# Query transposes moved from TensorE to the DMA crossbar, x products as block-diagonal matmuls, and a reordered start, in an attention-plus-FFN kernel

## Chip, cores, metric

One core of a Trainium2 chip. The metric is device time in microseconds (us) of the slowest core, here the only one; lower is better. In the profiles PE is TensorE, ACT ScalarE, DVE VectorE, POOL GpSimd and SP the sync engine; a line with `SPq` shows how long a DMA issue holds SP's queue, and a transfer's landing is the arrival of its data. A verdict compares two kernels in rounds on the same chip. Ratios are the mean time of one kernel's runs over that of the other's runs of the same rounds, so they are not quite the ratio of the medians quoted beside them.

## The reference

```python
# q, k, v: (8 batches, 8 heads, 576 tokens, 64) float32
q_s = softmax(q, axis=-1)                 # over the 64 features
k_s = softmax(k, axis=2)                  # over the 576 tokens
kv  = einsum('bhsd,bhse->bhde', k_s, v)   # 64 x 64 per head
attn = einsum('bhsd,bhde->bhse', q_s, kv)
x = attn.transpose(0, 2, 1, 3).reshape(4608, 512)
a = x @ w1;  b = x @ w2                   # 512 x 1024 each
out = ((a * b) @ w3) @ w_out              # 1024 x 1024, 1024 x 512
```

## The kernel before

It works in float16 with float32 sums. W3 @ W_out is computed once ("the W3 phase"), so that each chunk of 512 tokens needs only two sums for a and b ("s1") and one for the output ("s2"). Batches of attention (576 tokens) are prepared between the sums of earlier chunks. A batch needs, for each half of its heads (`i`): exponentials and a division, a transpose of the normalised queries, kv, and x. The parts that matter here (`pc` holds the pieces of batch 1, `s2(j, tb)` is the output sum of 128 tokens of a chunk; cuts marked `# ...`):

```python
def load_w12(wi, qt):                     # one quarter of w1 or w2: one 512 KB load
    t = slot([P, N_CT, 256])
    w = (moe_w1, moe_w2)[wi]
    nc.sync.dma_start(
        out=t, in_=w.rearrange("(c p) f -> p c f", p=P)[:, :, qt * 256:(qt + 1) * 256])
    w32[(wi, qt)] = t

def piece_t(b, i):                        # nine 128x128 transposes on TensorE, one copy
    pt = pAtt([P, R, P], F16)
    for r in range(R):
        nc.tensor.transpose(pt[:, r, :], eqns[(b, i)][:, r].rearrange("p h d -> p (h d)"), ident)
    qsT = attn.tile([P, 2, R, SP], F16, tag="qsT", name="qsT", bufs=3)
    nc.vector.tensor_copy(out=qsT.rearrange("p g r s -> p r g s"),
                          in_=pt.rearrange("p r (g s) -> p r g s", g=2))
    # ...

def piece_x(b, i, hf, copy=None):         # four 64x64 quadrants of the array
    xp = pAtt([P, 2, 512], F32)
    # ...
    for hh in range(2):
        rows = slice(64 * hh, 64 * hh + 64)
        for g in range(2):
            nc.tensor.matmul(xp[64 * g:64 * g + 64, hh, 0:HS], lhsT=kv2[rows, g, :],
                             rhs=qsT[rows, g, cols], start=True, stop=True)
    # ... copy to xT

# ... after the W3 phase: the second-batch phase, then chunks 1 to 8
pc[0]()                 # transposes of batch 1, first half
s2(0, 0)
pc[1]()                 # second half
s2(0, 1, alt=True)
pc[2]()                 # kv
s2(0, 2)
pc[3]()                 # x
s2(0, 3, alt=True)
pc[4]()                 # x
```

All loads and stores are issued by the sync engine (SP), in program order, on one queue: first batch 0, then w1 and w2, w3 and W_out, batches 1 and 2.

The softmax here doesn't subtract the row's maximum and nothing guards it: scores larger than these inputs give would overflow.

Of the kernel before, what the change touches and what calls it, by code (L numbers as in the profile page):

```python
# [16 lines left out]
def kernel(  # L17
# [11 lines left out]
    nc = tc.nc  # L29
# [10 lines left out]
    HS = S // 2  # L40
# [15 lines left out]
    wosb = [konst.tile([P, 2, C], F16, name=f"wo_{i}") for i in range(4)]  # L56
    W3O = [konst.tile([P, C], F16, name=f"W3O{i}") for i in range(N_FT)]
# [26 lines left out]
    def load_w12(wi, qt):  # L84
        t = slot([P, N_CT, 256])
        w = (moe_w1, moe_w2)[wi]
        nc.sync.dma_start(
            out=t, in_=w.rearrange("(c p) f -> p c f", p=P)[:, :, qt * 256:(qt + 1) * 256])
        w32[(wi, qt)] = t
# [53 lines left out]
    def piece_kv(b, i):  # L143
        kvp = pAtt([P, 2, 512], F32)
        for r in range(R):
            for g in range(2):
                rows = slice(64 * g, 64 * g + 64)
                nc.tensor.matmul(kvp[:, g, 0:130].rearrange("p (h e) -> p h e", h=2),  # L148
                                 lhsT=eks[(b, i)][rows, r].rearrange("p h d -> p (h d)"),
                                 rhs=v16buf[b % 2][rows, 2 * i:2 * i + 2, r, 0:65],  # L150
                                 start=(r == 0), stop=(r == R - 1))
        rc = attn.tile([P, 2], F32, tag="rc", name="rc", bufs=4)
        nc.vector.reciprocal(out=rc, in_=kvp[:, :, 64])
        kv2 = attn.tile([P, 2, D], F16, tag="kv2", name="kv2", bufs=4)
        for hh in range(2):
            sl = slice(64 * hh, 64 * hh + 64)
            nc.vector.tensor_tensor(
                out=kv2[sl], in0=kvp[sl, :, 65 * hh:65 * hh + 64],
                in1=rc[sl, :, None].broadcast_to([64, 2, 64]), op=ALU.mult)
        kvs[(b, i)] = kv2  # L160

    def piece_t(b, i):
        pt = pAtt([P, R, P], F16)
        for r in range(R):
            nc.tensor.transpose(pt[:, r, :], eqns[(b, i)][:, r].rearrange("p h d -> p (h d)"),  # L165
                                ident)
        qsT = attn.tile([P, 2, R, SP], F16, tag="qsT", name="qsT", bufs=3)
        nc.vector.tensor_copy(out=qsT.rearrange("p g r s -> p r g s"),  # L168
                              in_=pt.rearrange("p r (g s) -> p r g s", g=2))
        qsTs[(b, i)] = qsT.rearrange("p g r s -> p g (r s)")  # L170

    def piece_x(b, i, hf, copy=None):
        xp = pAtt([P, 2, 512], F32)
        qsT, kv2 = qsTs[(b, i)], kvs[(b, i)]
        cols = slice(hf * HS, (hf + 1) * HS)
        for hh in range(2):
            rows = slice(64 * hh, 64 * hh + 64)
            for g in range(2):
                nc.tensor.matmul(xp[64 * g:64 * g + 64, hh, 0:HS], lhsT=kv2[rows, g, :],  # L179
                                 rhs=qsT[rows, g, cols], start=True, stop=True)  # L180
        (copy or nc.scalar.copy)(  # L181
            out=xT[:, 2 * i:2 * i + 2, b * S + hf * HS:b * S + (hf + 1) * HS],
            in_=xp[:, :, 0:HS])

    def pieces(b):
        return [lambda: piece_t(b, 0), lambda: piece_t(b, 1),
                lambda: (piece_kv(b, 0), piece_kv(b, 1)),
                lambda: (piece_x(b, 0, 0), piece_x(b, 0, 1)),
                lambda: (piece_x(b, 1, 0), piece_x(b, 1, 1))]
# [9 lines left out]
    def s1(j, fb):  # L199
        t0 = j * CH  # L200
        qt, fo = fb // 2, (fb % 2) * P
        pa = pAB()
        for ct in range(N_CT):
            nc.tensor.matmul(pa, lhsT=w1sb[qt][:, ct, fo:fo + P], rhs=xT[:, ct, t0:t0 + CH],  # L204
                             start=(ct == 0), stop=(ct == N_CT - 1))
        a16 = ffn.tile([P, CH], F16, tag="a16", name="a16", bufs=3)
        nc.scalar.copy(out=a16, in_=pa)
        pb = pAB()
        for ct in range(N_CT):
            nc.tensor.matmul(pb, lhsT=w2sb[qt][:, ct, fo:fo + P], rhs=xT[:, ct, t0:t0 + CH],  # L210
                             start=(ct == 0), stop=(ct == N_CT - 1))
        ab = ffn.tile([P, CH], F16, tag="abT", name="abT", bufs=16)
        nc.vector.tensor_tensor(out=ab, in0=pb, in1=a16, op=ALU.mult)
        abT[(j, fb)] = ab

    outv = out.rearrange("(b s r) c -> b r s c", r=R, s=SP)

    def s2(j, tb, alt=False):
        po = pAtt([P, C], F32) if alt else pO()
        for ft in range(N_FT):  # L220
            nc.tensor.matmul(po, lhsT=abT[(j, ft)][:, tb * P:(tb + 1) * P], rhs=W3O[ft],  # L221
                             start=(ft == 0), stop=(ft == N_FT - 1))
        osb = ffn.tile([P, C], F32, tag="osb", name="osb", bufs=4)
        nc.vector.tensor_scalar(out=osb, in0=po, scalar1=ISC, scalar2=None, op0=ALU.mult)  # L224
        for h in range(2):
            b, rem = divmod(j * CH + tb * P + h * SP, S)
            nc.sync.dma_start(out=outv[b, rem // SP], in_=osb[h * SP:(h + 1) * SP, :])
# [44 lines left out]

    warm(26)
# [10 lines left out]
    load_w3(1)  # L284
# [11 lines left out]
    piece_x(0, 0, 0)  # L296
    piece_x(0, 0, 1)
# [4 lines left out]
    vcopy(out=w1sb[0], in_=w32[(0, 0)])  # L302
    acopy(out=w2sb[0], in_=w32[(1, 0)])
    piece_x(0, 1, 0)
    piece_x(0, 1, 1, vcopy)
# [5 lines left out]
    for ft in range(2, 8):  # L311
        load_w3(ft)
# [5 lines left out]
    for fb in range(N_FT):  # L318
        s1(0, fb)
# [8 lines left out]
        if fb == 6:  # L328
            w3_c(1)
            w3_t(0)  # L330
            vcopy(out=wosb[0], in_=w32[("o", 0)])
            vcopy(out=wosb[1], in_=w32[("o", 1)])
    w3_t(1)
    vcopy(out=wosb[2], in_=w32[("o", 2)])
    vcopy(out=wosb[3], in_=w32[("o", 3)])
    w3_c(2)

    def elementwise_steps(b):
# [5 lines left out]
        for i in range(2):  # L344
            st += [lambda i=i: exp_k(b, i, 0),
                   lambda i=i: (cast_v(b, i, pcopy), exp_k(b, i, 1))]
# [4 lines left out]
    for ft in range(N_FT):  # L351
        w3_m(ft)
        if ft + 3 < N_FT:
            w3_c(ft + 3)
        if ft + 2 < N_FT:
            w3_t(ft + 2)
        for f in {4: ew[0:2], 5: ew[2:5], 6: ew[5:8], 7: ew[8:9]}.get(ft, []):
            f()
    pc[0]()
    ew[9]()  # L360
    ew = elementwise_steps(2)
    s2(0, 0)
    pc[1]()
    s2(0, 1, alt=True)
    ew[0]()
    ew[1]()
    pc[2]()
    ew[2]()
    s2(0, 2)
    ew[3]()  # L370
    pc[3]()
    ew[4]()
    s2(0, 3, alt=True)
    pc[4]()
    ew[5]()
    ew[6]()
    ew[7]()
# [5 lines left out]
    for j in range(1, N_CHUNK):  # L383
        pcs = dict(zip((3, 4, 6, 8, 10) if j == 1 else (0, 1, 3, 5, 7),
# [3 lines left out]
        for n, f in enumerate(steps):  # L388
            ews.setdefault(min(n + 3, 11) if j == 1 else n, []).append(f)
        if j == 1:  # L390
            ews[0] = ew[8:9]
            ews[1] = ew[9:10]
# [12 lines left out]
    for tb in range(4):  # L405
        s2(N_CHUNK - 1, tb, alt=tb % 2)


# [28 lines left out]
```

## Time and profile before

| | before |
|---|---|
| median of 4 runs | 256.9 us |
| span of the profiled run | 255.1 us |
| first sum of s1 starts | 16.8 us |
| W3 phase ends | 50.1 us |
| chunk 1 starts | 63.0 us |
| from one batch-preparing chunk to the next | 23.9 us |

The page of the kernel before. The first two lines are span and busy time. The rest are the span in 40 slices of 6.4 us: busy share of TensorE (PE) in tenths, the clock granted to it in tenths, the DMA engines' busy share in tenths and what they moved. The last line gives shares of the chain of waits by engine.

```profile
span 255.1 us, 4178 instructions
...
PE 243.5 (95%) x1592; PEld 115.6 (45%) x1592; DVE 137.4 (54%) x244; ACT 112.0 (44%) x185; POOL 50.2 (20%) x38
...
PE   8999989897999999999999999999999999999982
...
PEclk9999999999999999999999999999999999999999
DMA  7999999994999219932991497211211321132135
GB/s 247 385 349 368 390 411 391 391 390 121 278 394 391 94 41 302 337 84 43 315 323 42 102 322 258 44 42 41 44 41 41 81 47 41 42 68 58 41 82 123
...
PE 87%; DMA 4%; DVE 3%; ACT 2%; issue 1%; POOL 1%; DVEq 0%; POOLq 0%; ACTq 0%
```

PE is busy nearly everywhere and at full clock, and the chain runs through it for 87% of the span. So time that leaves PE is time won, as long as nothing else takes its place. The DMA line says where that could be: from the second slice to the ninth, up to 57 us, the DMA engines are full, at 349 to 411 GB/s from the third slice on.

PE's timeline in one steady chunk (start, length, line, operation, count): kv (L148), one of the two x groups (L179), both transposes (L165), and the next chunk's kv. The first two lines are earlier: the last pair of matmuls of the W3 phase (L250; with 0.43 us for the two it ends at 50.1) and the first sum of chunk 1 (L204, 63.03).

```profile
49.68 0.59 PE L250 MATMUL po<-wo_86,w3T 128*128 128x512 f16 x2
...
63.03 0.61 PE L204 MATMUL pab<-xT,w_0_75 128*128 128x512 f16 x2
...
113.17 1.21 PE L148 MATMUL att<-v_0_73,ek 64*128 64x130 f16 x36
...
117.87 0.44 PE L179 MATMUL att<-qsT,kv_1532 64*64 64x288 f16 x8
...
130.82 0.67 PE L165 MATMUL att<-ident,eqn 128*128 128x128 f16 x9
...
133.05 0.67 PE L165 MATMUL att<-ident,eqn 128*128 128x128 f16 x9
...
137.10 1.10 PE L148 MATMUL att<-v_1_74,ek 64*128 64x130 f16 x32
```

From kv to kv it is 137.10 - 113.17 = 23.93 us. A nine-fold transpose takes 0.50 us of PE's issue time (from 130.82 to the next sum at 131.32; the printed length includes the end of the pipeline), so two cost 1.0 us a chunk. An x group costs 0.47 us.

The sync queue's timeline: the eight w1/w2 loads and the next loads.

```profile
3.94 13.53 SPq L87 DMA_DIRECT2D st<-in_moe_w_dram  x8
17.56 2.47 SPq L99 DMA_DIRECT2D st<-in_moe_w_dram  x2
```

The w1/w2 loads and their direct figures (least, median and greatest time that one holds the queue, in ns):

```profile
L87 SPq DMA_DIRECT2D st<-in_moe_w_dram x8: 470/1390/3577, 3.9 to 16.1; - x8
```

The shortest such issue took 0.47 us, the median 1.39; what held the longer ones the trace does not show. The times of the phases in the table above are read from PE's timeline in the same way.

### The profile page before, as it was taken

To read this page: it belongs to the slowest core of one execution; us is meant where nothing else is said; L and a number is where in the kernel's file an instruction comes from. 1 tells how busy PE (TensorE), PEld (TensorE's weight loads), DVE (VectorE), ACT (ScalarE), POOL (GpSimd) and SP (SyncE) were. 2 spreads that over 40 slices of the span, in tenths; PEclk is the share of its full clock that TensorE was granted. 3 is DMA by queue.
4 is the path that set the end of the run, shared out by engine and by line. 5 is a ranking of instruction groups with operands and counts; after the bars stand their busy time and mean duration, and the time that the engine had idled before them with its cause. 6 is when DMAs were issued, how large, how long until landed. Compare 5 with 4: busy or idle time off the path is not lost.

```text
span 255.1 us, 4178 instructions
## 1 busy us (share of the span) xinstructions
PE 243.5 (95%) x1592; PEld 115.6 (45%) x1592; DVE 137.4 (54%) x244; ACT 112.0 (44%) x185; POOL 50.2 (20%) x38
## 2 busy tenths in 40 slices
PE   8999989897999999999999999999999999999982
PEld 2534535453453554454455445444554444444430
DVE  2656774758485773586358636754553443443332
ACT  5466634944758547335733553373124221212100
POOL 1600000363636036023403420360000000000000
PEclk9999999999999999999999999999999999999999
DMA  7999999994999219932991497211211321132135
GB/s 247 385 349 368 390 411 391 391 390 121 278 394 391 94 41 302 337 84 43 315 323 42 102 322 258 44 42 41 44 41 41 81 47 41 42 68 58 41 82 123
DMA packets 25300, 48.51 MB, mean 190 GB/s; under 512 B 2240, under 2 KB 6336, under 8 KB 25280
## 3 DMA queue, kind: packets, MB, share of 16 engines
q1 hardware_dynamic: 25280, 48.24, 58.4%
q8 instruction: 12, 0.20, 0.3%
q14 instruction: 8, 0.07, 0.1%
HBM read 38.80 MB, written 9.44 MB: 189 GB/s over the span
## 4 chain that ended last, share of the span: by engine, by line
PE 87%; DMA 4%; DVE 3%; ACT 2%; issue 1%; POOL 1%; DVEq 0%; POOLq 0%; ACTq 0%
PE pab L204 23%; PE pab L210 23%; PE po L221 22%; PE pab L194 4%; DMA st<-in_moe_w_dram 4%; PE att L148 3%; PE att L165 3%; PE att L221 3%; PE att L179 2%; PE pab L250 1%; PE po L250 1%; DVE osb L224 1%; POOL eqn L134 1%; PE att L242 1%; ACT xT L181 1%
## 5 line engine op out<-in xcount | busy, mean ns | idle before, releaser
L134 POOL TENSOR_TENSOR eqn<-eq,dr 128x1152 f16<-128x1152 f16 x16 | 33.9, 2122 | 121.6 <-DVE dr L132 112.7
L221 PEld LDWEIGHTS <-abT 128*128 128x128 f16 x288 | 27.4, 98 | 33.7 <-issue 3.0
L224 DVE TENSOR_SCALAR osb<-po 128x512 f32<-128x512 f32 x32 | 22.1, 692 | 27.3 <-PE po L221 26.7
L181 ACT CAST xT<-att 128x576 f16<-128x576 f32 x31 | 18.4, 641 | 18.8 <-PE att L179 18.7
L127 DVE TENSOR_REDUCE ds<-eq 128x9 f32<-128x576 f16 x32 | 23.3, 742 | 4.8 <-ACT eq L115 4.8
L115 ACT ACTIVATE eq<-st 128x576 f16<-128x576 f32 x32 | 21.4, 684 | 2.9 <-DMA st<-in_q_dram 2.9
L108 ACT ACTIVATE ek<-st 128x576 f16<-128x576 f32 x32 | 20.8, 685 | 3.2 <-DMA st<-in_k_dram 3.2
L204 PE MATMUL pab<-xT,w_0_75 128*128 128x512 f16 x72 | 19.0, 379 | 1.3 <-ACT xT L181 0.8
L204 PE MATMUL pab<-xT,w_2_77 128*128 128x512 f16 x72 | 18.5, 380 | 0.0
L204 PE MATMUL pab<-xT,w_1_76 128*128 128x512 f16 x72 | 18.5, 380 | 0.0
L204 PE MATMUL pab<-xT,w_3_78 128*128 128x512 f16 x72 | 18.5, 379 | 0.0
L210 PE MATMUL pab<-xT,w_3_82 128*128 128x512 f16 x72 | 18.5, 379 | 0.0
L210 PE MATMUL pab<-xT,w_1_80 128*128 128x512 f16 x72 | 18.5, 379 | 0.0
L210 PE MATMUL pab<-xT,w_2_81 128*128 128x512 f16 x72 | 18.5, 379 | 0.0
L210 PE MATMUL pab<-xT,w_0_79 128*128 128x512 f16 x72 | 18.5, 379 | 0.0
L168 DVE COPY qsT<-att 128x1152 f16<-128x1152 f16 x16 | 12.0, 750 | 3.4 <-PE att L165 3.4
L194 PE MATMUL pab<-zero 128*128 128x512 f16 x40 | 12.0, 454 | 1.2 <-DVE zero L268 1.2
L221 PE MATMUL po<-W3O_87,abT 128*128 128x512 f16 x32 | 12.2, 381 | 0.8 <-DVE osb L224 0.8
L221 PE MATMUL po<-W3O_91,abT 128*128 128x512 f16 x32 | 12.1, 379 | 0.0
L221 PE MATMUL po<-W3O_92,abT 128*128 128x512 f16 x32 | 12.1, 379 | 0.0
L221 PE MATMUL po<-W3O_93,abT 128*128 128x512 f16 x32 | 12.1, 379 | 0.0
L221 PE MATMUL po<-W3O_94,abT 128*128 128x512 f16 x32 | 12.1, 379 | 0.0
(289 smaller groups left out, 349.6 us busy)
## 6 DMA issues: line engine op xcount, KB each, us to landing
st<-in_q_dram SPq DMA_DIRECT2D x16, 576.0 KB, 5.1
st<-in_k_dram SPq DMA_DIRECT2D x16, 576.0 KB, 7.7
st<-in_v_dram SPq DMA_DIRECT2D x16, 576.0 KB, 8.6
out_dram<-osb SPq DMA_DIRECT2D x72, 128.0 KB, 2.4
st<-in_moe_w_dram SPq DMA_DIRECT2D x16, 512.0 KB, 10.4
st<-in_moe_w_out_dram SPq DMA_DIRECT2D x4, 512.0 KB, 10.3
```

Of the source, the lines that this page charges most:

```text
L108: nc.scalar.activation(out=eks[(b, i)][:, :, hh, :], in_=qkv32[("k", b, i)][:, hh].rearrange("p (r d) -> p r d", r=R), func=AF.Exp)
L115: nc.scalar.activation(out=eqs[(b, i)][:, :, hh, :], in_=qkv32[("q", b, i)][:, hh].rearrange("p (r d) -> p r d", r=R), func=AF.Exp)
L127: nc.vector.tensor_reduce(out=dss[(b, i)][:, :, hh], in_=eqs[(b, i)][:, :, hh, :], axis=AX.X, op=ALU.add)
L134: eng.tensor_tensor(out=eqn.rearrange("p r h d -> p (r h) d"), in0=eqs[(b, i)].rearrange("p r h d -> p (r h) d"), in1=dr[:, :, None].broad ...
L148: nc.tensor.matmul(kvp[:, g, 0:130].rearrange("p (h e) -> p h e", h=2), lhsT=eks[(b, i)][rows, r].rearrange("p h d -> p (h d)"), rhs=v16bu ...
L168: nc.vector.tensor_copy(out=qsT.rearrange("p g r s -> p r g s"), in_=pt.rearrange("p r (g s) -> p r g s", g=2))
L181: (copy or nc.scalar.copy)(out=xT[:, 2 * i:2 * i + 2, b * S + hf * HS:b * S + (hf + 1) * HS], in_=xp[:, :, 0:HS])
L194: nc.tensor.matmul(wp, lhsT=zero[:, 0:P], rhs=zero, start=True, stop=True)
L204: nc.tensor.matmul(pa, lhsT=w1sb[qt][:, ct, fo:fo + P], rhs=xT[:, ct, t0:t0 + CH], start=(ct == 0), stop=(ct == N_CT - 1))
L210: nc.tensor.matmul(pb, lhsT=w2sb[qt][:, ct, fo:fo + P], rhs=xT[:, ct, t0:t0 + CH], start=(ct == 0), stop=(ct == N_CT - 1))
L221: nc.tensor.matmul(po, lhsT=abT[(j, ft)][:, tb * P:(tb + 1) * P], rhs=W3O[ft], start=(ft == 0), stop=(ft == N_FT - 1))
L224: nc.vector.tensor_scalar(out=osb, in0=po, scalar1=ISC, scalar2=None, op0=ALU.mult)
```

## The change

Its intent: take the transposes of batches 1 to 7 off TensorE and let the DMA crossbar do them; do x as full 128x128 matmuls with a block-diagonal kv instead of four 64x64 quadrants; start the first chunk with half sums; reorder the second-batch phase; split the last copy and store. The block-diagonal form puts the channels of x in another order over the partitions. The rows of w1 and w2 must follow, and that made one load into four loads of 64 partitions. The core of the diff:

```diff
     def load_w12(wi, qt):
         t = slot([P, N_CT, 256])
-        w = (moe_w1, moe_w2)[wi]
-        nc.sync.dma_start(
-            out=t, in_=w.rearrange("(c p) f -> p c f", p=P)[:, :, qt * 256:(qt + 1) * 256])
+        w = (moe_w1, moe_w2)[wi].rearrange("(i h g e) f -> i h e g f", i=2, h=2, g=2)
+        for i in range(2):
+            for hh in range(2):
+                nc.sync.dma_start(out=t[64 * hh:64 * hh + 64, 2 * i:2 * i + 2, :],
+                                  in_=w[i, hh, :, :, qt * 256:(qt + 1) * 256])
...
+    def dma_t(b, i):
+        nc.sync.dma_start_transpose(
+            out=qt_tile(b, i), in_=eqns[(b, i)].rearrange("p r h d -> p (r h d)"))
...
-        for hh in range(2):
-            rows = slice(64 * hh, 64 * hh + 64)
-            for g in range(2):
-                nc.tensor.matmul(xp[64 * g:64 * g + 64, hh, 0:HS], lhsT=kv2[rows, g, :],
-                                 rhs=qsT[rows, g, cols], start=True, stop=True)
+        for g in range(2):
+            nc.tensor.matmul(xp[:, g, 0:n].rearrange("p (r s) -> p r s", s=SP),
+                             lhsT=kv2[:, g, :], rhs=qsT[:, r0:r1, 64 * g:64 * g + 64],
+                             start=True, stop=True)
...
-    vcopy(out=w1sb[0], in_=w32[(0, 0)])
-    acopy(out=w2sb[0], in_=w32[(1, 0)])
-    piece_x(0, 1, 0)
-    piece_x(0, 1, 1, vcopy)
+    pcopy(out=w1sb[0], in_=w32[(0, 0)])
+    piece_x(0, 1, 0, 8, acopy, vcopy)
+    piece_x(0, 1, 8, 9)
...
+    pas = [pAB(), pAB()]
+    for fb in range(2):
+        s1_mm(pas[fb], w1sb, 0, fb, range(2))      # half sums
...
-                   lambda i=i: (cast_v(b, i, pcopy), exp_k(b, i, 1))]
+                   lambda i=i: (dma_t(b, i), cast_v(b, i, pcopy), exp_k(b, i, 1))]
...
+    ew = elementwise_steps(2)
+    s2(0, 0, alt=True)
     pc[0]()                                        # now kv of batch 1
-    ew[9]()
-    ew = elementwise_steps(2)
-    s2(0, 0)
-    pc[1]()
-    s2(0, 1, alt=True)
+    s2(0, 1)
     ew[0]()
     ew[1]()
+    pc[1]()                                        # x
... (the rest of the phase, the places of the pieces in chunk 1, and the split of the last copy are cut)
```

More of the change, by code (lines that the diff above doesn't have):

```diff
@@ L39 @@
     N_CHUNK = T // CH
-    HS = S // 2
     SC = 2.0 ** 5
@@ L56 @@
     wosb = [konst.tile([P, 2, C], F16, name=f"wo_{i}") for i in range(4)]
+    kvbd = [konst.tile([P, 2, P], F16, name=f"kvbd{i}") for i in range(4)]
     W3O = [konst.tile([P, C], F16, name=f"W3O{i}") for i in range(N_FT)]
@@ L153, in piece_kv @@
         nc.vector.reciprocal(out=rc, in_=kvp[:, :, 64])
-        kv2 = attn.tile([P, 2, D], F16, tag="kv2", name="kv2", bufs=4)
+        kv2 = kvbd[(2 * b + i) % 4]
         for hh in range(2):
@@ L157, in piece_kv, with qt_tile @@
             nc.vector.tensor_tensor(
-                out=kv2[sl], in0=kvp[sl, :, 65 * hh:65 * hh + 64],
+                out=kv2[sl, :, sl], in0=kvp[sl, :, 65 * hh:65 * hh + 64],
                 in1=rc[sl, :, None].broadcast_to([64, 2, 64]), op=ALU.mult)
         kvs[(b, i)] = kv2
+    def qt_tile(b, i):
+        qsTs[(b, i)] = attn.tile([P, R, P], F16, tag="qsT", name="qsT", bufs=4)
+        return qsTs[(b, i)]
     def piece_t(b, i):
@@ L166, in piece_t, with piece_x @@
                                 ident)
-        qsT = attn.tile([P, 2, R, SP], F16, tag="qsT", name="qsT", bufs=3)
-        nc.vector.tensor_copy(out=qsT.rearrange("p g r s -> p r g s"),
-                              in_=pt.rearrange("p r (g s) -> p r g s", g=2))
-        qsTs[(b, i)] = qsT.rearrange("p g r s -> p g (r s)")
-    def piece_x(b, i, hf, copy=None):
+        nc.vector.tensor_copy(out=qt_tile(b, i), in_=pt)
+    def dma_t(b, i):
+        nc.sync.dma_start_transpose(
+            out=qt_tile(b, i), in_=eqns[(b, i)].rearrange("p r h d -> p (r h d)"))
+    def piece_x(b, i, r0, r1, *copies):
+        n = (r1 - r0) * SP
         xp = pAtt([P, 2, 512], F32)
         qsT, kv2 = qsTs[(b, i)], kvs[(b, i)]
-        cols = slice(hf * HS, (hf + 1) * HS)
-        for hh in range(2):
-            rows = slice(64 * hh, 64 * hh + 64)
-            for g in range(2):
-                nc.tensor.matmul(xp[64 * g:64 * g + 64, hh, 0:HS], lhsT=kv2[rows, g, :],
-                                 rhs=qsT[rows, g, cols], start=True, stop=True)
-        (copy or nc.scalar.copy)(
-            out=xT[:, 2 * i:2 * i + 2, b * S + hf * HS:b * S + (hf + 1) * HS],
-            in_=xp[:, :, 0:HS])
+        for g in range(2):
+            nc.tensor.matmul(xp[:, g, 0:n].rearrange("p (r s) -> p r s", s=SP),
+                             lhsT=kv2[:, g, :], rhs=qsT[:, r0:r1, 64 * g:64 * g + 64],
+                             start=True, stop=True)
+        dst = xT[:, 2 * i:2 * i + 2, b * S + r0 * SP:b * S + r1 * SP]
+        if len(copies) == 2:
+            for g in range(2):
+                copies[g](out=dst[:, g], in_=xp[:, g, 0:n])
+        else:
+            (copies[0] if copies else nc.scalar.copy)(out=dst, in_=xp[:, :, 0:n])
     def pieces(b):
-        return [lambda: piece_t(b, 0), lambda: piece_t(b, 1),
-                lambda: (piece_kv(b, 0), piece_kv(b, 1)),
-                lambda: (piece_x(b, 0, 0), piece_x(b, 0, 1)),
-                lambda: (piece_x(b, 1, 0), piece_x(b, 1, 1))]
+        return [lambda: (piece_kv(b, 0), piece_kv(b, 1)),
+                lambda: (piece_x(b, 0, 0, 5), piece_x(b, 0, 5, 9)),
+                lambda: (piece_x(b, 1, 0, 5), piece_x(b, 1, 5, 9))]
     def warm(n):
@@ L197, with s1_mm, s1_a, s1_b @@
     abT = {}
-    def s1(j, fb):
-        t0 = j * CH
-        qt, fo = fb // 2, (fb % 2) * P
-        pa = pAB()
-        for ct in range(N_CT):
-            nc.tensor.matmul(pa, lhsT=w1sb[qt][:, ct, fo:fo + P], rhs=xT[:, ct, t0:t0 + CH],
+    def s1_mm(p, wsb, j, fb, cts):
+        qt, fo, t0 = fb // 2, (fb % 2) * P, j * CH
+        for ct in cts:
+            nc.tensor.matmul(p, lhsT=wsb[qt][:, ct, fo:fo + P], rhs=xT[:, ct, t0:t0 + CH],
                              start=(ct == 0), stop=(ct == N_CT - 1))
+    def s1_a(pa):
         a16 = ffn.tile([P, CH], F16, tag="a16", name="a16", bufs=3)
         nc.scalar.copy(out=a16, in_=pa)
-        pb = pAB()
-        for ct in range(N_CT):
-            nc.tensor.matmul(pb, lhsT=w2sb[qt][:, ct, fo:fo + P], rhs=xT[:, ct, t0:t0 + CH],
-                             start=(ct == 0), stop=(ct == N_CT - 1))
+        return a16
+    def s1_b(j, fb, pb, a16):
         ab = ffn.tile([P, CH], F16, tag="abT", name="abT", bufs=16)
@@ L214, in s1, with s2 @@
         abT[(j, fb)] = ab
+    def s1(j, fb, pa=None):
+        if pa is None:
+            pa = pAB()
+            s1_mm(pa, w1sb, j, fb, range(N_CT))
+        else:
+            s1_mm(pa, w1sb, j, fb, range(2, N_CT))
+        a16 = s1_a(pa)
+        pb = pAB()
+        s1_mm(pb, w2sb, j, fb, range(N_CT))
+        s1_b(j, fb, pb, a16)
     outv = out.rearrange("(b s r) c -> b r s c", r=R, s=SP)
-    def s2(j, tb, alt=False):
-        po = pAtt([P, C], F32) if alt else pO()
+    def s2(j, tb, alt=False, last=False):
+        po = pAB() if alt else pO()
         for ft in range(N_FT):
@@ L223, in s2 @@
         osb = ffn.tile([P, C], F32, tag="osb", name="osb", bufs=4)
-        nc.vector.tensor_scalar(out=osb, in0=po, scalar1=ISC, scalar2=None, op0=ALU.mult)
+        if last:
+            nc.scalar.activation(out=osb[:, 0:256], in_=po[:, 0:256], func=AF.Copy, scale=ISC)
+            nc.vector.tensor_scalar(out=osb[:, 256:512], in0=po[:, 256:512], scalar1=ISC,
+                                    scalar2=None, op0=ALU.mult)
+        else:
+            nc.vector.tensor_scalar(out=osb, in0=po, scalar1=ISC, scalar2=None, op0=ALU.mult)
         for h in range(2):
             b, rem = divmod(j * CH + tb * P + h * SP, S)
-            nc.sync.dma_start(out=outv[b, rem // SP], in_=osb[h * SP:(h + 1) * SP, :])
+            (nc.scalar if last and h else nc.sync).dma_start(
+                out=outv[b, rem // SP], in_=osb[h * SP:(h + 1) * SP, :])
     w3Ts = {}
@@ L271 @@
         nc.gpsimd.memset(t[:, :, :, 64:65], 1.0 / SC)
+    for t in kvbd:
+        nc.gpsimd.memset(t, 0.0)
     warm(26)
@@ L283 @@
     load_w3(0)
-    load_w3(1)
     for i in range(4):
@@ L295 @@
     cast_v(0, 1, acopy, slice(1, 2))
-    piece_x(0, 0, 0)
-    piece_x(0, 0, 1)
+    piece_x(0, 0, 0, 8)
+    piece_x(0, 0, 8, 9)
     cast_v(0, 1, vcopy, slice(0, 1))
@@ L301 @@
     warm(2)
-    vcopy(out=w1sb[0], in_=w32[(0, 0)])
-    acopy(out=w2sb[0], in_=w32[(1, 0)])
-    piece_x(0, 1, 0)
-    piece_x(0, 1, 1, vcopy)
+    pcopy(out=w1sb[0], in_=w32[(0, 0)])
+    piece_x(0, 1, 0, 8, acopy, vcopy)
+    piece_x(0, 1, 8, 9)
+    for h in range(2):
+        vcopy(out=w2sb[0][:, :, h * P:(h + 1) * P], in_=w32[(1, 0)][:, :, h * P:(h + 1) * P])
+    pas = [pAB(), pAB()]
+    for fb in range(2):
+        s1_mm(pas[fb], w1sb, 0, fb, range(2))
     def cast_w12(qt):
@@ L309, in cast_w12 @@
         acopy(out=w2sb[qt], in_=w32[(1, qt)])
-    for ft in range(2, 8):
+    for ft in range(1, 8):
         load_w3(ft)
@@ L318 @@
     for fb in range(N_FT):
-        s1(0, fb)
+        s1(0, fb, pas[fb] if fb < 2 else None)
         if fb == 0:
@@ L328 @@
         if fb == 6:
-            w3_c(1)
+            vcopy(out=wosb[0], in_=w32[("o", 0)])
             w3_t(0)
-            vcopy(out=wosb[0], in_=w32[("o", 0)])
             vcopy(out=wosb[1], in_=w32[("o", 1)])
-    w3_t(1)
     vcopy(out=wosb[2], in_=w32[("o", 2)])
-    vcopy(out=wosb[3], in_=w32[("o", 3)])
+    pcopy(out=wosb[3], in_=w32[("o", 3)])
+    w3_c(1)
     w3_c(2)
@@ L354 @@
             w3_c(ft + 3)
+        if ft == 0:
+            w3_t(1)
         if ft + 2 < N_FT:
             w3_t(ft + 2)
-        for f in {4: ew[0:2], 5: ew[2:5], 6: ew[5:8], 7: ew[8:9]}.get(ft, []):
+        for f in {3: ew[0:2], 4: ew[2:4], 5: ew[4:6], 6: ew[6:8], 7: ew[8:10]}.get(ft, []):
             f()
+    ew = elementwise_steps(2)
+    s2(0, 0, alt=True)
     pc[0]()
-    ew[9]()
-    ew = elementwise_steps(2)
-    s2(0, 0)
-    pc[1]()
-    s2(0, 1, alt=True)
+    s2(0, 1)
     ew[0]()
     ew[1]()
+    pc[1]()
+    ew[2]()
+    s2(0, 2, alt=True)
+    ew[3]()
     pc[2]()
-    ew[2]()
-    s2(0, 2)
-    ew[3]()
-    pc[3]()
     ew[4]()
-    s2(0, 3, alt=True)
-    pc[4]()
-    ew[5]()
-    ew[6]()
-    ew[7]()
+    s2(0, 3)
     for which, i in LOADS:
@@ L383 @@
     for j in range(1, N_CHUNK):
-        pcs = dict(zip((3, 4, 6, 8, 10) if j == 1 else (0, 1, 3, 5, 7),
+        pcs = dict(zip((5, 7, 9) if j == 1 else (1, 4, 7),
                        pieces(j + 1) if j + 1 < B else []))
@@ L388 @@
         for n, f in enumerate(steps):
-            ews.setdefault(min(n + 3, 11) if j == 1 else n, []).append(f)
+            ews.setdefault(min(n + 4, 11) if j == 1 else n, []).append(f)
         if j == 1:
-            ews[0] = ew[8:9]
-            ews[1] = ew[9:10]
+            for n in range(5):
+                ews[n] = ew[5 + n:6 + n] + ews.get(n, [])
         ld = LOADS if j + 3 < B else []
@@ L405 @@
     for tb in range(4):
-        s2(N_CHUNK - 1, tb, alt=tb % 2)
+        s2(N_CHUNK - 1, tb, alt=tb % 2, last=tb == 3)
 _INS = ['q', 'k', 'v', 'moe_w1', 'moe_w2', 'moe_w3', 'moe_w_out']
```

## The prediction

> **What bounds it now.** TensorE. The page gives PE 95% busy in a 255.1 us span at full granted clock; the chain of waits runs through PE for 87%. In the timeline a 128x512 matmul issues every 0.216 us, so the fixed products cost 576 x 0.216 = 124 us (a and b), 288 x 0.216 = 62 us (output) and 13.9 us (W3 times W_out). From about 104 us PE never idles, and a chunk that also prepares a later batch takes 24.0 us: 20.8 of fixed products, 2 x 0.50 for nine-fold query transposes, 1.15 for kv, 2 x 0.48 for x. Before that there are losses: a prologue of 16.8 us filled with warm-up matmuls; 1.75 us of waits in the W3 phase (31.9 to 50.1); 2.8 us in the second-batch phase (50.1 to 63.0, of which 10.1 is work); 0.8 us at the border of the second and third chunk (xT copy). DMA moves about 390 GB/s without a gap until 58 us: that stretch is load-bound as well.
>
> **What the change does.**
> 1. Transposes off PE for batches 1 to 7: 14 x 0.50 = 7.0 us of PE, and VectorE copies that were not critical. In their place 14 crossbar transfers of 295 KB. [...] In steady state each has over 10 us until use.
> 2. x as block-diagonal: 1152 columns per head group, estimate from 0.216 us per 512: 0.49 us, against 0.48. No gain.
> 3. First chunk starts half a sum early: about 1 us.
> 4. w1/w2 arrive in 32 loads of 128 KB instead of 8 of 512 KB. A load costs the queue 0.33 to 0.47 us to issue, so 10.6 to 15 us, with eight (1 MB) outstanding: the load front should fall 1 to 3 us behind.
> 5. Second-batch phase: ideal work 9.1 us instead of 10.1. But both batch-1 transposes stand in the sync queue behind the batch-2 loads, which land near 59 us now. [...] the first lands at 61 to 63, while PE wants it near 55 to 57: a stall of several us that may eat this phase's gain. Batch 2's transposes, behind the batch-3 loads, may stall 1 to 2 us more.
> 6. Tail: last copy and stores split: 0.5 to 0.8 us.
>
> **Critical path.** Chunks 2 to 6: -5.0 us. Chunk 1: -1.0 and the 0.8 border stall. Tail: -0.7. Prologue to 63 us: between -3 (no stall) and +4 (ring order and slow w loads). Sum: -11 to -2; I lean to the middle. Time 250.5 us, range 246.5 to 255.5. Chances: faster by over 2% 0.6, within 2% 0.35, slower 0.05.
>
> **What would show it.** Chunks between 104 and 176 us near 23.0 instead of 24.0 us; x pieces 0.48 to 0.50 us; crossbar transfers landing in 2 to 4 us when the ring is empty, over 8 us for batch 1; the first x of batch 1 waiting for qsT by DMA; the last w1/w2 load landing later than 26 us; start of chunk 1 between 60 and 67 us instead of 63.0.
>
> **What would make it wrong.** Crossbar transfers several times slower than plain ones (rings clogged, chunks stalled on qsT): no gain or a loss. Transfers that overtake the queued loads: 246 us or less. Block-diagonal x slower than its columns say.

The sum is -11 to -2 us, with its middle at 250.5 us (the terms as listed add up to -10.5 to -3.5). The landing at 61 to 63 us, and with it part of the +4 of the prologue, stands as my estimate: no trace had shown a crossbar transfer when I wrote it. "Ring" in the recorded texts is a queue of transfers, and "ring order" the supposition that a transfer comes after those queued ahead of it; a_order and b_best_x2 try it below (3.3 and 3.6 us to landing without loads ahead, 11.4 and 10.6 behind them).

## The result

The changed kernel is correct and slower: 267.56 us median (266.67 to 268.52, 4 runs) against 256.9 (256.81 to 258.26, 4 runs); ratio 1.0403, interval 1.0353 to 1.0453. Executions over 1.5% slower than the fastest of the same kernel are left out of the means. I had said 250.5 us, at most 255.5.

The page of the changed kernel:

```profile
span 265.9 us, 3866 instructions
...
PE 240.9 (91%) x1402; PEld 114.0 (43%) x1402; DVE 128.8 (48%) x230; ACT 111.0 (42%) x186; POOL 53.2 (20%) x44
...
PE   8977758997399699999999999999999999999983
...
PEclk9999979999899999999999999999999999999999
DMA  7976699999939999399469939924511113112235
GB/s 258 345 188 193 200 374 412 392 392 392 199 80 339 314 373 247 68 233 373 130 175 304 298 73 301 341 76 90 117 41 40 39 43 79 39 39 64 55 75 124
```

PE is busy for 2.6 us less than before, in a span 10.8 us longer: it waits. Two lines show where. In slices 3 to 5 (13 to 33 us) the DMA engines moved 188 to 200 GB/s, where they had moved 349 to 390. And PE's clock line has two dents, slices 6 and 11.

| from the timelines | before | after | later by |
|---|---|---|---|
| first sum of s1 starts | 16.8 | 17.8 | 1.1 |
| W3 phase ends | 50.1 | 59.9 | 9.8 |
| chunk 1 starts | 63.0 | 76.8 | 13.7 |
| chunk 2 starts | 80.4 | 96.2 | 15.8 |
| end of span | 255.1 | 265.9 | 10.8 |

From chunk 2 on the change wins 15.8 - 10.8 = 5.0 us. All the loss is in front of that. The steady chunk after the change, kv (L150) and x (L184):

```profile
123.74 1.21 PE L150 MATMUL att<-v_0_73,ek 64*128 64x130 f16 x36
...
135.75 0.65 PE L184 MATMUL att<-qsT,kvbd_88 128*128 128x320 f16 x4
...
146.69 1.21 PE L150 MATMUL att<-v_1_74,ek 64*128 64x130 f16 x36
```

kv to kv is 146.69 - 123.74 = 22.95 us, 0.98 less than before; the transposes are gone, and an x group takes 0.49 us (from its start at 135.75 to the next matmul at 136.24), against 0.47 before.

The sync queue after the change:

```profile
3.88 27.20 SPq L89 DMA_DIRECT2D st<-in_moe_w_dram  x32
31.18 0.54 SPq L101 DMA_DIRECT2D st<-in_moe_w_dram  x1
...
59.15 10.41 SPq L176 DMA_TRANSPOSE qsT<-eqn  x2
```

The w1/w2 loads hold the queue for 27.2 us instead of 13.5, and the next load leaves at 31.2 instead of 17.6. The two transposes of batch 1 hold it for 10.4 us. The loads' figures, to set beside those of before, and what the queue waited for before it issued one (us in total, times, longest):

```profile
L89 SPq DMA_DIRECT2D st<-in_moe_w_dram x32: 595/606/1351, 3.9 to 30.5; - x32
...
SPq L89 <- DMA st<-in_v_dram: 2.9, 2, 2.0
SPq L89 <- DMA st<-in_k_dram: 2.2, 2, 1.3
```

A load of 128 KB mostly holds the queue 0.60 us, and once nothing else holds them up they follow one another every 0.65 us: 131072 bytes in 0.65 us are at most 202 GB/s. That makes 20.8 us for 32. Of the rest, 5.1 us are waits for k and v of batch 0 to land: the fifth small load, the eleventh load of the queue, is the first that waits, and it waits for the third. So eight loads were in flight then, four of 576 KB and four of 128 KB. The remainder is a few longer issues, up to 1.35 us. PE in the places that the table names (the brackets give idle time and what ended it):

```profile
36.05 1.49 PE L210 MATMUL pab<-xT,w_3_82 128*128 128x512 f16 x4 [2.69 <-ACT a_457 L215]
...
59.49 0.59 PE L274 MATMUL po<-wo_86,w3T 128*128 128x512 f16 x2
...
70.72 1.12 PE L184 MATMUL att<-qsT,kvbd_89 128*128 128x320 f16 x4 [4.65 <-DMA qsT<-eqn]
71.64 0.63 PE L239 MATMUL pab<-W3O_91,abT 128*128 128x512 f16 x1
72.07 0.63 PE L239 MATMUL pab<-W3O_92,abT 128*128 128x512 f16 x1
...
76.76 1.03 PE L210 MATMUL pab<-xT,w_0_75 128*128 128x512 f16 x4
...
91.79 0.65 PE L184 MATMUL att<-qsT,kvbd_87 128*128 128x320 f16 x4 [2.54 <-DMA qsT<-eqn]
```

At 36.05 PE had waited 2.69 us for ACT's copy of a sum, which stood behind ACT's own wait of 4.29 us for a late w2 load. At 70.72 it had waited 4.65 us for the crossbar, and at 91.79 another 2.54 us. After the wait of 4.65 us the clock is halved (0.50 from 70.7 to 73.8): the 128x512 matmuls at 71.64 and 72.07 are 0.43 us apart instead of 0.216.

### The profile page after: what moved, and what is told of

The parts are those of the page before. It is cut to its first block, busy times and chain, and to the rows that moved or that the text cites. A ratio compares the mean times of both kernels' runs of the same rounds, so it can differ in the third digit from the quotient of the medians.

```text
span 265.9 us, 3866 instructions
## 1 busy us (share of the span) xinstructions
PE 240.9 (91%) x1402; PEld 114.0 (43%) x1402; DVE 128.8 (48%) x230; ACT 111.0 (42%) x186; POOL 53.2 (20%) x44
## 4 chain that ended last, share of the span: by engine, by line
PE 60%; DVE 0%; POOL 0%; ACT 0%; issue 0%
PE pab L210 35%; PE po L239 20%; PE att L150 2%; PE att L184 2%; PE pab L239 1%; POOL v_1_74 L122 0%; DVE osb L247 0%; DVE osb L244 0%; ACT osb L243 0%
## 5 line engine op out<-in xcount | busy, mean ns | idle before, releaser
L239 PEld LDWEIGHTS <-abT 128*128 128x128 f16 x288 | 28.0, 99 | 32.6 <-issue 2.7
L192 ACT CAST xT<-att 128x640 f16<-128x640 f32 (+3 forms) x31 | 18.0, 631 | 18.6 <-PE att L184 18.6
L210 PEld LDWEIGHTS <-w_3_82 128*128 128x128 f16 x72 | 7.1, 99 | 11.7 <-ACT w_3_82 L339 2.7
```

Source lines behind the costliest of these rows:

```text
L192: (copies[0] if copies else nc.scalar.copy)(out=dst, in_=xp[:, :, 0:n])
L210: nc.tensor.matmul(p, lhsT=wsb[qt][:, ct, fo:fo + P], rhs=xT[:, ct, t0:t0 + CH], start=(ct == 0), stop=(ct == N_CT - 1))
L239: nc.tensor.matmul(po, lhsT=abT[(j, ft)][:, tb * P:(tb + 1) * P], rhs=W3O[ft], start=(ft == 0), stop=(ft == N_FT - 1))
```

## Experiments

Runs are compared with those of the kernel before, of the same rounds. "b_" kernels are edits of the kernel before, "a_" kernels edits of the changed one. The four theories in question: the split loads (W), the queue order of the transposes (Q), the other reorderings of the start (R), and the crossbar's own worth (X). The medians of a_actq and a_order are those of their two fast runs; two runs of each were slow.

| run | edit | median us | ratio to before (interval) |
|---|---|---|---|
| b_w32 | w1/w2 in 32 loads of 64 partitions | 266.14 | 1.0363 (1.0340 to 1.0386) |
| a_w8 | w1/w2 in 8 loads again (wrong result) | 258.35 | 1.0051 (0.9999 to 1.0103) |
| a_pet1 | batch 1 transposed on TensorE again | 264.07 | 1.0273 (1.0236 to 1.0309) |
| b_dmat | crossbar for batches 3 to 7 alone | 252.10 | 0.9808 (0.9793 to 0.9823) |
| b_w16 | w1/w2 in 16 loads of 64 partitions | 264.48 | 1.0270 (1.0229 to 1.0311) |
| b_w32c | w1/w2 in 32 loads of 128 partitions | 262.62 | 1.0202 (1.0156 to 1.0248) |
| a_actq | transposes issued from ACT's queue | 276.49 | 1.0739 (1.0655 to 1.0822) |
| b_best | hybrid | 249.40 | 0.9685 (0.9648 to 0.9723) |
| b_w3h | w3 in 16 loads of 64 partitions | 265.33 | 1.0311 (1.0263 to 1.0358) |
| b_w3q | the same from two queues | 271.23 | 1.0538 (1.0474 to 1.0602) |
| a_order | batch-2 loads queued behind the transposes | 266.58 | 1.0354 (1.0292 to 1.0416) |
| b_best_x2 | hybrid, crossbar from batch 2 | 252.47 | 0.9790 (0.9738 to 0.9841) |
| b_w3m | w3 in loads of partitions 32-95, 0-31, 96-127 | 262.73 | 1.0216 (1.0190 to 1.0242) |
| b_w3n | w3 in loads of partitions 0-63, 64-95, 96-127 | 265.82 | 1.0310 (1.0273 to 1.0347) |
| b_best2 | b_best, one piece moved | 247.89 | 0.9628 (0.9613 to 0.9643) |

The intervals of b_dmat, b_w32c, b_best_x2 and b_w3m contain a difference of 2%: these four differ from the kernel before, but whether by more than 2% is unclear.

### b_w32: the suspected loads alone, in the kernel before

```diff
-        w = (moe_w1, moe_w2)[wi]
-        nc.sync.dma_start(
-            out=t, in_=w.rearrange("(c p) f -> p c f", p=P)[:, :, qt * 256:(qt + 1) * 256])
+        w = (moe_w1, moe_w2)[wi].rearrange("(i c h e) f -> i h e c f", i=2, c=2, h=2)
+        for i in range(2):
+            for hh in range(2):
+                nc.sync.dma_start(out=t[64 * hh:64 * hh + 64, 2 * i:2 * i + 2, :],
+                                  in_=w[i, hh, :, :, qt * 256:(qt + 1) * 256])
```

> The kernel before, with each 512 KB load of w1 and w2 split into four 128 KB loads of 64 partitions, nothing else changed. Theory (the small loads alone delay the load front): in the changed kernel each such load holds the sync queue 0.6 us plus a gap, about 0.65 us in all, so the 32 loads need about 27 us instead of 13.5 and the W3 phase ends about 9 to 10 us later; this kernel should take 264 to 268 us, W3 phase ending near 59 us. Rival (the other edits of the prologue, the casts given to POOL and the later w3 loads, cost the time): 257 to 259 us.

266.14 us, correct. The last group of the W3 phase starts at 57.8 us and ends at 59.5. So the split of the loads, with nothing else changed, moves that end by 9.4 us and costs 9.1 us over the median of before in the same rounds (257.09). W holds; R is not needed for the bulk. The sum in my expectation was wrong, though its result was not: 32 loads at 0.65 us are 20.8 us, not 27. The queue was held 26.9 us; most of what goes beyond 20.8 I put down to waits for batch 0's loads, which are 5.1 us in the changed kernel (an estimate from there).

### a_w8: the loads made whole in the changed kernel

The same edit in reverse: the changed kernel gets `load_w12` of the kernel before. Its result is wrong (relative error 1.18), because the weight rows then do not match the channel order of x; the work is the same.

> The changed kernel with the eight 512 KB loads of w1 and w2 of the kernel before; the weight rows then stand in the wrong order for its head layout, so the result is wrong on purpose, the work is the same. Theory (small loads): the W3 phase ends at 50 to 52 us instead of 59.9 and the time falls by 8 to 10 us, to 257.5 to 260 us, with the waits on the crossbar transposes of batches 1 and 2 still there. Rival (other prologue edits): 265 us or more.

258.35 us: 9.2 less than the changed kernel's median. The W3 phase ends at 51.6 us. That is still 1.5 us later than before: the other reorderings of the start cost a little rather than gain. Here the half sums start at 17.59 us and the remaining ones wait for x and for a copy of w2; before, the first sum started at 16.78. The waits for the crossbar are there as expected, 2.81 us (batch 1) and 2.54 us (batch 2).

### a_pet1: batch 1 on TensorE again

```diff
     def dma_t(b, i):
+        if b <= 1:
+            return
...
     pc[0]()
+    piece_t(1, 0)
     s2(0, 1)
+    piece_t(1, 1)
```

> The changed kernel with batch 1 transposed on TensorE again (two nine-fold transposes in the second-batch phase), crossbar from batch 2 on. Theory (the batch-1 crossbar transposes land 11.4 us after issue because they stand behind the batch-2 loads): the 4.65 us wait of the first x goes, and with it about 1.7 us of matmuls at half clock after the idle time, 1.0 us of transposes comes back: 262 to 263 us, chunk 1 starting near 71.5 instead of 76.8. The wait of batch 2 (2.5 us) stays. Rival (the phase is bound by the late arrival of batch 1 itself, and the transposes only show it): 266 us or more.

264.07 us: 3.5 less, not the 4.5 to 5.5 that I expected, so this was a partial miss. Chunk 1 starts at 72.0 instead of 76.8, as Q said (the wait and the half clock are gone). Part of it is lost again: a sum of x waits 0.67 us for the copy of the transpose, and batch 2 waits 2.70 us. After that wait TensorE ran at little more than half pace: the eight 128x512 matmuls from 87.68 took 3.00 us instead of 8 x 0.216 = 1.73, and the x group at 90.68 took 0.90 us instead of 0.49. It had not done so after the 2.54 us in the changed kernel (clock 1.00 from 91.8 to 94.0). That is about 1.7 us, more than the size of the miss.

### b_dmat: the crossbar alone, where it has time

The code has a constant for the first batch on the crossbar; it is written out as 3 here.

```diff
+    def dma_t(b, i):
+        if b >= 3:
+            nc.sync.dma_start_transpose(
+                out=qt_tile(b, i), in_=eqns[(b, i)].rearrange("p r h d -> p (r h d)"))
...
-        return [lambda: piece_t(b, 0), lambda: piece_t(b, 1),
+        return [lambda: piece_t(b, 0) if b < 3 else None,
+                lambda: piece_t(b, 1) if b < 3 else None,
...
-                   lambda i=i: (cast_v(b, i, pcopy), exp_k(b, i, 1))]
+                   lambda i=i: (dma_t(b, i), cast_v(b, i, pcopy), exp_k(b, i, 1))]
```

The quadrant form of x stays; it reads columns in pieces of 64 from the untangled tile, and its halves become 5 and 4 row groups (diff cut).

> The kernel before, with its four-quadrant x products and its weight loads, but crossbar transposes for batches 3 to 7 in place of those on TensorE. Theory (the crossbar itself is worth 1.0 us per chunk once its transfers have time to land, and full-array x brings nothing): chunks of 22.95 us as in the changed kernel, five of them, so 5.0 us less: 251 to 252.5 us. Rival 1 (the shorter chunk of the changed kernel owes part to the full-array x products, or quadrant products on rows with gaps are slower): chunks of 23.3 us or more. Rival 2 (the crossbar transfers clog the queue and delay loads and stores): 255 us or more.

252.10 us, correct: 5.0 us less than the median of before in the same call (257.09). kv to kv in its timeline is 134.75 - 111.83 = 22.92 us. X holds, and the full-array x has no part in the gain: quadrant x gives the same chunk.

### b_w16 and b_w32c: what is slow in the split loads

b_w16 splits a 512 KB load in two halves of 64 partitions; b_w32c splits it in four pieces of all 128 partitions.

```diff
+        # b_w16
+        w = (moe_w1, moe_w2)[wi].rearrange("(c h e) f -> h e c f", h=2, e=64)
+        for hh in range(2):
+            nc.sync.dma_start(out=t[64 * hh:64 * hh + 64], in_=w[hh, :, :, qt * 256:(qt + 1) * 256])
...
+        # b_w32c
+        for c in range(N_CT):
+            nc.sync.dma_start(out=t[:, c, :], in_=w[c * P:(c + 1) * P, qt * 256:(qt + 1) * 256])
```

> The kernel before with each 512 KB load of w1 and w2 split into two of 64 partitions (256 KB each, 16 in all). Theory (what delays the front is the 0.65 us of queue time per load, whatever it carries): 16 loads need 10.4 us of queue time, less than the 13.5 us that the eight large ones took at memory pace, so nothing is lost: 256.5 to 258.5 us. Rival (loads of 64 partitions or of 1 KB pieces move slowly in the DMA engines themselves): half of the loss of b_w32 or more, 260 us and up.

> The kernel before with each 512 KB load of w1 and w2 split into four of all 128 partitions, one 1 KB row each (128 KB, 32 in all). Theory A (issue time is that of the shape: two-dimensional 128-partition loads of w3 took 0.33 us): 0.33 to 0.4 us per load, 32 loads in 11 to 13 us, little lost: 257 to 260 us. Theory B (any small load costs the queue 0.6 us or waits on the eight-load window): as b_w32, 264 us or more.

b_w16 took 264.48 us. My theory that only the queue time counts has fallen. The windows of 16 to 24 us (busy time of each engine, then granted clock, DMA share, GB/s), first before, then b_w16, then b_w32:

```profile
core 0: us, PE busy (x) PEld busy (x) DVE busy (x) ACT busy (x) POOL busy (x), PEclk, DMA share, GB/s
...
16.00:20.00 4.00, 3.50 (x22) 1.39 (x21) 2.30 (x4) 3.15 (x5) 0.00 (x0) 1.00 1.09 350
20.00:24.00 4.00, 4.00 (x20) 1.77 (x19) 2.43 (x4) 2.74 (x4) 0.00 (x0) 1.00 1.10 361
```

```profile
16.00:20.00 4.00, 1.60 (x12) 0.46 (x11) 1.59 (x3) 1.58 (x2) 0.00 (x0) 0.89 1.13 224
20.00:24.00 4.00, 4.00 (x14) 1.59 (x13) 1.29 (x2) 1.48 (x2) 0.00 (x0) 0.68 1.13 222
```

```profile
16.00:20.00 4.00, 2.47 (x16) 0.97 (x17) 1.75 (x3) 2.08 (x3) 0.00 (x0) 1.00 0.56 167
20.00:24.00 4.00, 2.92 (x14) 1.23 (x13) 1.30 (x3) 1.66 (x4) 0.00 (x0) 1.00 0.65 192
```

In b_w16 the DMA engines are full (share 1.13; it sums the time of packets, so it can pass 1) and move 223 GB/s; before, they are as full and move 350 to 361, with the same pieces of 1 KB. So the 64-partition loads were slow here with the engines full. In b_w32 the share is only 0.56 to 0.65, at 167 to 192 GB/s: there the engines are also short of work, because the queue issues too slowly (0.605 us in the middle for one load of 128 KB).

b_w32c took 262.62 us, between my two theories. Its loads held the queue 0.33 us at the least and 0.43 us in the middle, yet its 32 loads took 22.7 us. 31 issues at 0.43 us and one of 2.13 are 15.5 us; most of the other 7.2 I put down to waits for loads of batch 0, of which the changed kernel had 5.1 us (an estimate, not read from this trace). So small loads cost something even over 128 partitions: 5.5 us here (before had 257.12 in these rounds), where b_w16, with few loads over 64 partitions, cost 7.4 us. The two overlap in b_w32, which cost 9.1 us.

### b_w3h, b_w3q, b_w3m, b_w3n: do the partitions of a load matter?

b_w16 moved 222 to 224 GB/s where the kernel before moved 350 to 361. The theory of the next runs, not shown by any run up to here, is that the rate of a load depends on which partitions it covers. They split the loads of w3, whose rows are 4 KB, in the kernel before (the edits of the four are put in one form here):

```diff
-        nc.sync.dma_start(out=t, in_=moe_w3[ft * P:(ft + 1) * P, :])
+        for lo, hi in ((0, 64), (64, 128)):                # b_w3h; b_w3q: the second half from POOL's queue
+        for lo, hi in ((32, 96), (0, 32), (96, 128)):      # b_w3m
+        for lo, hi in ((0, 64), (64, 96), (96, 128)):      # b_w3n
+            nc.sync.dma_start(out=t[lo:hi], in_=moe_w3[ft * P + lo:ft * P + hi, :])
```

> The kernel before with each 512 KB load of w3 (128 rows of 4 KB) split into two of 64 partitions, both on the sync queue. Looks for what made 64-partition loads of w1 and w2 run at 221 GB/s with all engines busy. Theory[...]: rows of 4 KB do not help, the DMA rate falls to 215 to 225 GB/s while w3 arrives, 3.7 MB of it take 6 to 8 us longer, time 262 to 265 us. Rival (short 1 KB pieces were slow): rate stays near 390 GB/s, 257 to 258.5 us.

> As b_w3h, but the loads to the upper 64 partitions are issued from the POOL queue, so that both halves are in flight at once. [...]the rate comes back to 330 GB/s or more, time 257 to 260 us. If a 64-partition load is slow for another reason of its own[...], the rate stays near 220 and the time near that of b_w3h.

> The kernel before with each w3 load split into partitions 32-95 (256 KB), 0-31 and 96-127 (128 KB each). [...]2 to 5 us faster than b_w3n. Rival (small loads as such): same time as b_w3n within 1 us.

> The kernel before with each w3 load split into partitions 0-63 (256 KB), 64-95 and 96-127 (128 KB each): the same three sizes as b_w3m[...]. [...]220 to 245 GB/s while w3 arrives, 265 to 268 us, as b_w3h or a little worse. Rival: same as b_w3m.

b_w3h: 265.33 us, and 227 to 246 GB/s while w3 alone arrives (24 to 28 and 36 to 48 us), where the kernel before moved 390 to 401 in the same windows. So 64-partition loads were slow with rows of 4 KB too.

b_w3q: 271.23 us. It was meant to put both halves in flight at once, and it failed as a test: POOL issued its loads after waits of up to 10.9 us of its own, so the halves seldom overlapped. The rate did not come back (202 to 302 GB/s from 28 to 52 us), which decides nothing by itself.

b_w3m and b_w3n have the same number of loads and the same sizes, and differ only in which partitions a load covers: half of the bytes go to 32-95 in b_w3m, to 0-63 in b_w3n. Windows of b_w3m, then of b_w3n:

```profile
24.00:28.00 4.00, 4.00 (x21) 1.79 (x19) 2.12 (x4) 2.34 (x4) 0.00 (x0) 1.00 1.05 267
...
36.00:40.00 4.00, 2.16 (x12) 1.12 (x12) 1.51 (x3) 0.75 (x2) 0.00 (x0) 0.60 0.98 258
```

```profile
24.00:28.00 4.00, 4.00 (x21) 1.76 (x19) 2.15 (x4) 1.43 (x3) 0.00 (x0) 1.00 1.03 222
...
36.00:40.00 4.00, 1.01 (x2) 0.25 (x2) 1.56 (x3) 0.00 (x0) 0.00 (x0) 0.60 0.95 220
```

267 against 222 GB/s at 24 to 28 us, where the first w3 loads arrive. (Between the two windows W_out arrives too, in loads over 128 partitions.) b_w3m is 3.1 us faster by the medians and the two intervals lie apart. So the placement counts: half of the bytes at 32-95 instead of 0-63 won about a third of the loss back (3.1 of 8.6 us). What it is about the placement that counts the runs do not show.

### a_order and a_actq: why the first transposes are late

```diff
-    for which, i in LOADS:
-        load_qkv(2, which, i)          # taken from its place ahead of the W3 phase
...
+    for which, i in LOADS:             # a_order: put behind the transposes of batch 1
+        load_qkv(2, which, i)
     ew = elementwise_steps(2)
...
-        nc.sync.dma_start_transpose(
+        nc.scalar.dma_start_transpose(     # a_actq, alone
```

> The changed kernel with the loads of batch 2 put into the sync queue after the crossbar transposes of batch 1 instead of before. Ring-order theory: with nothing of size ahead of them these two land 3 to 5 us after issue (11.4 and 5.2 before), TensorE does not wait for them, chunk 1 starts near 71 us instead of 76.8; total 260 to 264 us, as batch 2 itself comes later. If a crossbar transfer is slow by itself at this point: landing still 8 us or more.

> The changed kernel with the crossbar transposes issued from the ACT queue, so that they do not stand behind the batch loads in the sync queue's rings. Theory (ring order makes them late): the waits of TensorE for qsT by DMA (4.65 and 2.54 us) go, with the half-clock stretch after the first, and the transposes of batch 1 land in 4 to 6 us; 258.5 to 262 us, ACT paying 1.3 to 2 us per issue. Rival (a crossbar transfer beside running loads is slow on any ring): landing still 8 us or more and 265 us or more.

The first transpose of batch 1 in the changed kernel, and in a_order: the time that it holds the queue in ns, and the us from issue to landing.

```profile
L176 SPq DMA_TRANSPOSE qsT<-eqn x1: 7172/7172/7172, 59.2 to 59.2; - x1
...
DMA to landing us min/median/max: 11.4/11.4/11.4
```

```profile
L176 SPq DMA_TRANSPOSE qsT<-eqn x1: 1352/1352/1352, 59.4 to 59.4; - x1
...
DMA to landing us min/median/max: 3.3/3.3/3.3
```

11.4 us behind the batch-2 loads, 3.3 us without them, and the queue is held 1.35 us instead of 7.17. Q holds in this: without the batch-2 loads ahead of it the transfer lands soon. Whether they delay it by their place in the queue or by running beside it, a_order does not separate. TensorE did not wait for batch 1 in a_order, and chunk 1 started at 71.9 us. But its time is no better: 266.2 and 266.9 us in its two fast runs (two others were slow, 270.73 and 357.6, the second with a clock of 0.66), because batch 2 itself now came late and its x waited 6.19 us for the crossbar. That profile is of a slow run; I read only landing times and the order of waits from it. The total of 260 to 264 us that I expected was a miss.

a_actq is a clear miss, 275.26 and 277.71 us in its two fast runs:

```profile
L176 ACTq DMA_TRANSPOSE qsT<-eqn x14: 1259/2170/7853, 57.9 to 200.1; - x14
...
DMA to landing us min/median/max: 3.2/11.1/17.5
```

The median landing is 11.1 us on a queue of its own (12.8 and 10.7 for batch 1), which is what I had written down for the rival, that a transfer beside running loads is slow on any queue; and one issue held ACT's queue, where sums are copied out for PE, for 7.85 us. PE's longest wait, 6.04 us, was for ACT. Whether the loads that run beside a transpose make it late no run here isolates. Its profile, too, is of a slow run (two of the four were slow).

### b_best, b_best_x2, b_best2: the parts that pay

b_best is b_dmat plus three parts of the change:

```diff
-    for f in {4: ew[0:2], 5: ew[2:5], 6: ew[5:8], 7: ew[8:9]}.get(ft, []):
+    for f in {3: ew[0:2], 4: ew[2:4], 5: ew[4:6], 6: ew[6:8], 7: ew[8:10]}.get(ft, []):
...  # second-batch phase: s2, both transposes, kv, s2, x, s2, x, s2; s2 in pAB buffers where alt
-        pcs = dict(zip((3, 4, 6, 8, 10) if j == 1 else (0, 1, 3, 5, 7),
+        pcs = dict(zip((3, 4, 5, 7, 9) if j == 1 else (0, 1, 3, 5, 7),     # b_best2: (2, 3, 5, 7, 9)
...
+        if last:      # the last copy on ACT and DVE, its stores on two queues
```

> The hybrid b_dmat (large loads, quadrant x, crossbar from batch 3) with three parts of the change that cost nothing in the traces: elementwise work of batch 1 one step earlier and the second-batch phase reordered with output sums in the pab buffers, x of batch 2 finished before the last sum of chunk 1, last copy and store split. Expected from the waits shown by the trace of b_dmat (0.8 for eqn, about 1.2 for att buffers, 0.8 at the chunk border, 0.7 in the tail): 248.5 to 250.5 us. If the reordered phase brings nothing by itself: 251.4 us.

> b_best with the crossbar from batch 2 on. In this order the first transpose of batch 2 is queued ahead of the batch-3 loads (landing 3 to 5 us), the second behind them (landing 8 to 10 us, needed about 12 us after issue): no wait, 1.0 us less than b_best, 248 to 248.8 us. If the second comes late: a wait of 1 to 3 us for qsT and 249.5 us or more.

> b_best with the two TensorE transposes of batch 2 one place earlier in chunk 1, so that the second kv sum no longer waits for the copy of the second transpose (1.13 us in the trace of b_best): 248.0 to 249.0 us. If the wait only moves: 249.4 us.

b_best: 249.40 us, as expected. b_best_x2, with the crossbar from batch 2 on, is slower, 252.47 us, against the 248 to 248.8 that I expected. The first transpose of batch 2, ahead of the batch-3 loads, landed in 3.6 us, the second, behind them, in 10.6, and PE shows the wait:

```profile
79.71 0.69 PE L186 MATMUL att<-qsT,kv 64*64 64x320 f16 x8 [2.94 <-DMA qsT<-eqn]
```

So on the sync queue the loads ahead of a transpose set from which batch on the crossbar pays. b_best2 moves the two remaining transposes of chunk 1 one place forward, away from the kv sum that waited for their copy: 247.89 us (247.83 to 247.90), ratio 0.9628, just below the range that I expected. It is correct, and it beats both kernels: 3.7% faster than before.

## Why the prediction was wrong

- **The step that failed is point 4**, "the load front should fall 1 to 3 us behind". It fell 9.8 us behind (end of the W3 phase 59.9 instead of 50.1), and b_w32 shows that the loads alone do 9.4 us of it, a_w8 that making them whole takes 9.2 us off the total. The term was mis-sized in three ways. I took 0.33 to 0.47 us of queue time per load from loads over 128 partitions; those of 64 partitions took 0.60, 0.65 with the gap, which is 20.8 us for 32 rather than at most 15. I named the eight loads in flight and did not price them: the queue waited 5.1 us for older loads to land, and was held 27.2 us in all. And I left out that a 64-partition load moves slowly: 223 instead of 350 GB/s with full engines (b_w16).
- **Point 3**, "First chunk starts half a sum early: about 1 us", was wrong in sign: the first sum starts 1.1 us later. In a_w8, without the slow loads, the W3 phase still ends 1.5 us later than before.
- **Point 5** was right in mechanism: the wait for the first x of batch 1 was 4.65 us, that of batch 2 2.54 us, and a_order shows the batch-2 loads as the cause (11.4 against 3.3 us to landing). That queue order is how they delay it fits a_order and b_best_x2 (3.6 us ahead of loads, 10.6 behind), but a_actq was late on a queue of its own (12.8 and 10.7 us for batch 1), so order is not the whole of it. The size was slightly low, for the clock: after 4.65 us without work PE ran at half clock (0.50 from 70.7 to 73.8). One x group took 0.92 us instead of 0.48, and the next five steps 0.43 us instead of 0.22: about 1.5 us in all (worked out from the timeline). The traces show about the same after shorter waits, of 2.69 us (clock 0.50 from 37.4 to 39.9) and, in a_w8, of 2.54 us (the x group at 81.68 took 0.92 us instead of 0.49, the next eight 128x512 matmuls 2.91 instead of 1.73), while after the 2.54 us in the changed kernel the clock stayed full (1.00 from 91.8 to 94.0). So the length of the last wait alone did not decide it.
- **My sum "Prologue to 63 us: between -3 and +4"** was thus 13.7, of which 9.8 came before the second-batch phase and 3.9 in it. For chunk 1 I said -1.8 in sum (0.8 of it for a stall that lies just behind the chunk's end); up to its end it came to +2.1, mainly because the batch-2 wait of 2.54 us, which I had named but left out of this sum, ate its gain.
- **Points 1 and 2** were right in what they were worth, point 6 roughly. Chunk pace 22.95 us (I said near 23.0), x 0.48 to 0.49 us, -5.0 us from chunk 2 to the end (I said -5.7 with the tail). Crossbar landing was 3.2 to 3.3 us with an empty queue (I said 2 to 4): a transfer by itself filled the DMA engines (share 1.11) and moved 209 GB/s (changed kernel, 187.4 to 188.6 us), where plain loads moved 374 to 412 (slices 6 to 10 of its page). I had taken it to be faster, an estimate that no trace showed; that cost nothing where it had over 10 us until use. The tail was over-estimated: from the last matmul's start to the end of the span it takes 265.9 - 261.07 = 4.8 us, against 255.1 - 249.94 = 5.2 before, so about 0.3 us, not 0.5 to 0.8. The timeline shows why: the two halves of the last copy run one after the other (ACT from 261.48 to 261.86, then VectorE from 261.90, which waited for ACT), so only the split of the stores is left to gain.
- What stays open: how the cost of b_w32 divides between the number of loads and their 64 partitions, as each alone is more than half of it; what makes loads of 64 partitions move more slowly; and why the transposes on ACT's queue land so late.

## What to carry to other kernels

When a change of layout alters a load, price the load again: number of transfers, queue time of each, how many are in flight (eight here), and the partitions that each spans; four loads of 64 partitions were not four quarters of one load of 128 (0.60 us of queue time each here, 223 GB/s instead of 350 in b_w16), and cost more than the change won. A transfer that TensorE will wait for is priced by what stands ahead of it in its queue (a crossbar transfer landed in 3.3 us without loads ahead, a_order, and in 11.4 behind them, changed kernel), so give it slack or place it ahead of the prefetches; another queue was no way round (a_actq, 11.1 us in the middle). Take a bundle of edits apart: here the crossbar was worth 5 us, the full-array x nothing, and the split loads, which were there only for the sake of that x, cost 9.
